# Attention and soft mixture of experts on one core: the first peaks by TensorE, fewer heating products, another order of tasks, idle products in two waits

## The chip, the core and the metric

The kernel runs on one core of one Trainium2 chip. The core has TensorE (PE: products of matrices, with PEld for the loading of weights), VectorE (DVE), ScalarE (ACT), GpSimd (POOL) and SyncE (SP), which here issues nearly all DMA transfers; 16 DMA engines move the data between the device's memory (HBM) and the core's SBUF. TensorE writes its results into PSUM. Every engine takes its instructions in the order in which they stand, and waits where an operand isn't there or a buffer isn't free. The metric is the device time of one execution in microseconds.

## What is computed

Two steps, in fp32 at the borders. First attention over 8 batches and 8 heads, 576 positions of 64 elements, with rotary embedding; then a soft mixture of 8 experts with 4 slots each, over 4608 rows of 512 elements.

```
q_rot, k_rot = rotate(q), rotate(k)
scores = scale * q_rot @ k_rot.T
scores = scores - max(scores, axis=-1)
attn = exp(scores); attn /= sum(attn, -1) + 1e-9
out = attn @ v                       # [8, 8, 576, 64]

x = out, with heads side by side      # [4608, 512]
logits = x @ phi                      # 32 slots
d = softmax(logits, axis=0)           # over the rows
slot_input = d.T @ x                  # [8, 4, 512]
for e in range(8):
    slot_out[e] = relu(slot_input[e] @ w1[e]) @ w2[e]    # 512 -> 1024 -> 512
c = softmax(logits, axis=1)           # over the slots
result = c @ slot_out                 # [4608, 512]
```

## The kernel before

Heads go in pairs, two heads of 64 elements over the 128 partitions: 32 pairs p, four to a batch (NP = 4). A pair passes through some 45 tasks, each a Python function that issues a few instructions on its engines. Its x_in (queries and keys, two transfers of 576 KB, L247, `load0` and `load1`, two buffers) is multiplied with cosine and sine by GpSimd (`spin0`, `spin1`, L253, eight operations), added by VectorE (`join`, L257), cast to fp16 by ScalarE (`high0`, `high1`, L262), and VectorE subtracts the cast from the original (`low`, L270), so that a number is held as two fp16 parts, hl. `low` is the last reader of x_in, so it frees the buffer.

The scores are made twice. The first time only to find the largest of each row: `m0` to `m4` and `m_rem` (L300, L313) form products into PSUM and VectorE reduces them (L303, L315); `m_min` (L319) joins the parts to nm, the negated maxima, one row per partition. TensorE turns nm (`m_turn`, L325), ScalarE scales and casts it to mr (`m_half`, L335), and two small DMAs on SP lay mr out over two partitions of the tile peak (`m_rows`, L340, L341). There are two such tiles, for even and odd pairs. The second time, `t0` to `t4` and `t8` (L355, L368 to L370) form the scores out of both parts, and a product of peak and the constant lift subtracts the maxima in PSUM; ScalarE takes the exponentials (L358, L373). Then follow the products with the values (`av0` to `av10`, L411, L422), the copies out of PSUM (`o_out`, `o_down`), `recip`, `norm`, the turning of the normalized result (`natural`, copied by ScalarE in `natural_out`, L474), and the pair's part of the logits (`logits`, L481, L484, added up by VectorE, L493). Per batch there are tasks for the running maxima and the slots. TensorE has three PSUM slots in rotation for all these tasks (`bank2`).

What stands where on each engine comes from the tables WHEN (the pairs in the middle), FIRST (the first five) and LAST (the last four): `at` turns task and pair into a number, `line` sorts the numbers, and a loop calls the tasks in that order. So the order of the calls is the order on TensorE, VectorE and ScalarE. In the function called `first_rows`, the first pair's `m_rows` is followed on SP by the loads of pair 2, of phi and of sel.

Before the loop the kernel forms products that nobody reads, to keep TensorE at work while the first pair's data come: `heat(N_WARM)`, 17 products (L759) at the start, and `heat(N_HEAT)`, 12 more ahead of the first `m_turn`.

The experts' weights are 64 tiles of 512 KB (L612). Thirty go into a pool wp during the pairs (`weights`). The others wait for space: wx (five tiles) and wk and wh1, wh0 for the buffers of the pairs' inputs and of hl, wq (five tiles) for the buffers of the last pairs (`release_fore`; one of them is peak), wl (four tiles) for those of the attention (`release_att`). `trickle` issues the ones of wx, wk and wh. `steady` is the list of instructions whose place on SP and GpSimd is set by the program that gathers them; it is closed ahead of the last `trickle` loop. The remaining loads take tiles that the first layer of the experts has read.

Behind the last pair come its `norm`, `natural` and `logits`, the statistics, the update of the slots (TensorE products L821 to L865, with a few products of lift and lift, L818, whose numbers SPEND gives, in the waits), the first layer (L889, four blocks of 32 products, the first block over the tiles 0 to 7; tile 6 is that of wk), the second (L910), and the combination (L938, L939), whose 18 tiles of 512 KB are stored by SP (L941).

Of the kernel before, what the change touches and what calls it, by code (L numbers as in the profile page):

```python
# [7 lines left out]
F32 = mybir.dt.float32  # L8
# [36 lines left out]
SPEND = (0, 4, 2, 0, 6)  # L45
STEPS = (0, 0, 5, 0, 0, 5, 0, 0, 0)
N_WARM = 17
N_HEAT = 12
# [20 lines left out]
    "m_min": (-3.52783, -3.74988, -3.4456, -3.54521), "m_turn": (-2.65751, -3.22757, -2.90005, -2.93818),  # L69
    "m_half": (-2.47643, -2.32388, -2.50442, -2.74079), "m_rows": (-1.67456, -1.59636, -1.01091, -1.36182),  # L70
# [10 lines left out]
    "o_out": (3.92962, 3.94615, 3.87859, 3.96882), "o_down": (4.02285, 3.90092, 4.43108, 4.25105),  # L81
    "weights": (6.68793, 8.11001, 10.4734, 7.96367), "recip": (7.06685, 8.50895, 7.64337, 5.66094),
    "norm": (9.04517, 9.97761, 7.81794, 8.82978), "soft3": (10.71329, -1.23258, 22.11176, 22.86781),
    "natural": (11.03659, 10.57574, 10.30017, 9.50469), "natural_out": (11.0413, 10.59331, 11.08607, 9.87664),
    "logits": (11.6819, 12.18299, 11.9393, 11.08074), "logits_sum": (11.75168, 12.37214, 12.01238, 11.24891),
    "stat1": (14.20481, 16.70567, 26.85987, 14.34257), "soft2": (17.19783, 18.68756, 28.52708, 15.06539),
    "slots": (24.26839, 14.86922, -21.6337, 15.49421), "soft0": (29.66187, 31.16378, 41.9456, 13.09224),
    "stat0": (58.67023, 6.43439, 39.30635, 12.92594),
}
FIRST = {  # L90
    "m_rem": (-420.74199, -258.52084, -165.95497, -91.55186, -32.58086),
    "m0": (-416.09865, -286.81487, -140.59459, -101.97371, -50.62576),
    "m2": (-412.20094, -270.0157, -129.84012, -87.82755, -68.19657),
    "m3": (-403.90776, -262.95985, -149.84108, -109.9302, -38.36104),
    "m1": (-399.15564, -289.81588, -118.56698, -106.41711, -36.28915),
    "m4": (-389.35943, -247.90996, -158.73441, -94.61606, -57.50848),
    "m_min": (-377.37328, -241.64993, -117.64569, -87.38313, -27.82539),
    "join": (-377.36326, -348.95641, -243.7818, -151.58901, -94.91012),
    "m_turn": (-352.2095, -226.16715, -100.92287, -72.642, -26.10801),
    "m_half": (-349.91816, -225.0694, -96.54795, -70.71858, -22.59302),  # L100
    "low": (-346.40436, -295.64275, -150.94049, -69.26017, -71.53601),
    "m_rows": (-337.67967, -197.52355, -88.5627, -36.46158, -4.19543),
    "t8": (-314.59698, -151.13586, -85.2923, -25.75504, -0.50974),
    "t2": (-311.27385, -151.13883, -84.94182, -0.14828, -0.87715),
    "t0": (-285.00525, -136.70424, -61.87914, -32.66543, -2.39072),
    "soft0": (-267.48427, -201.24595, 3.73945, 13.40987, -248.89171),
    "av5": (-267.32619, -96.76236, -76.7603, 1.06239, 0.13262),
    "t1": (-261.10481, -138.41608, -84.62048, -0.67329, -1.38994),
    "load_v": (-259.92437, -147.90602, -94.1895, -72.03072, -5.71268),
    "av1": (-258.00393, -93.30542, -37.73087, -16.69992, 3.26102),  # L110
    "av10": (-248.07756, -85.59323, -27.88133, 2.16407, 3.9268),
    "soft1": (-235.02539, -134.85944, -322.53084, 20.01567, 1.89106),
    "high0": (-234.98804, -340.48244, -222.89928, -142.08461, -85.55401),
    "t3": (-230.41978, -121.38007, -60.9526, -22.48296, -3.97013),
    "t4": (-229.99713, -146.42219, -62.60678, -23.05545, -3.99833),
    "soft3": (-222.15667, 24.22066, -12.56887, 24.46301, -39.84925),
    "av3": (-197.83158, -112.42151, -73.01473, 1.26269, -0.18588),
    "av4": (-194.34117, -111.6644, -39.4965, 1.16011, 2.88299),
    "av7": (-193.53141, -102.7179, -34.84723, -13.08601, 0.91351),
    "av9": (-192.59135, -134.50116, -32.79874, -14.28511, 1.64504),  # L120
    "av0": (-185.07388, -88.05057, -39.19938, 0.99983, -0.12547),
    "av8": (-170.0289, -94.63629, -56.43594, -14.16475, 2.53229),
    "av2": (-168.0465, -130.44334, -56.1101, 1.41561, 1.66757),
    "av6": (-155.12663, -95.29877, -39.5128, -4.51807, 3.20444),
    "o_out": (-147.40069, -82.01871, -26.27853, 2.29791, 4.03845),
    "load0": (-141.97913, -25.42989, -149.95166, -283.06751, -158.47656),
    "o_down": (-136.55419, -81.65478, -26.47399, 2.44084, 4.1333),
    "weights": (-109.57446, 25.46476, 6.62982, -1.59969, -58.15807),
    "recip": (-102.27546, -58.4345, -7.54993, 2.78188, 4.50588),
    "spin1": (-93.90425, -414.42416, -264.72383, -160.57665, -110.78333),  # L130
    "soft2": (-93.41299, -315.28447, -101.43259, 21.6938, -17.79966),
    "norm": (-90.51137, -31.67471, 5.54815, 7.84989, 6.27133),
    "natural": (-69.97429, -27.4891, 8.73388, 9.34029, 10.87984),
    "natural_out": (-59.04176, -25.9581, 9.65759, 9.79417, 11.06854),
    "logits": (-43.36981, 3.87649, 9.8946, 11.1204, 14.12073),
    "logits_sum": (-43.2881, 4.82347, 10.33544, 11.30244, 14.2095),
    "stat0": (-36.38519, 17.61955, 9.89016, 13.35178, -409.00246),
    "spin0": (-21.4379, -398.65092, -288.22025, -246.63741, -156.13304),
    "load1": (-6.95274, -271.47629, -100.89511, -206.15958, -156.77186), "trickle0": 0.4431, "trickle1": 1.2621,
    "trickle2": 2.5296, "high1": (3.15516, -324.01766, -205.53181, -139.88352, -73.53007), "trickle3": 3.4658,  # L140
    "stat1": (13.43099, -353.9255, 23.26806, 14.22494, -112.62711),
    "slots": (25.91835, -21.11139, -68.31089, 17.77357, -247.82112),
}
LAST = {
# [32 lines left out]
def attn_softmoe(ctx, tc, qk, q0, v, phi, w, cs, ident, sel, seg, out):  # L177
# [43 lines left out]
    for t in peaks:  # L221
        nc.vector.memset(t, 0.0)
# [816 lines left out]
```

## Time and profile before

| what | value |
|---|---|
| median of 3 runs | 506.17 us (503.56 to 509.76) |
| the profiled execution | 507.91 us, its span 506.1 us |
| TensorE busy | 478.3 us, 95% of the span |
| VectorE busy | 362.5 us, 72% |
| ScalarE busy | 290.6 us, 57% |
| GpSimd busy | 265.4 us, 52% |
| moved by DMA | 93.96 MB, 186 GB/s over the span |

The times of the rows below are microseconds from the start of the span. A line of the timeline has the start, the duration, engine, line of the kernel and operation, output and inputs with the sizes, and how many instructions of that kind stand together; in brackets stands how long the engine was idle before them and for what it waited. "SPq" is the queue of SP, whose DMA issues count here. PEclk is the clock that TensorE was granted, as a share of 2.4 GHz.

### The profile page before, as it was taken

How to read it: one execution, taken by the hardware profiler on the slowest of the kernel's cores; microseconds unless marked ns; L12 is line 12 of the kernel's file. 1: busy time of each engine (PE TensorE's matmuls, PEld its weight loads, DVE VectorE, ACT ScalarE, POOL GpSimd, SP SyncE). 2: the span in 40 equal slices, each digit the busy share in tenths (PEclk: the TensorE clock that was granted, in tenths of full speed). 3: DMA queues.
4: the chain of work that ended last, by engine and by line, in shares of the span. 5: the costliest groups of instructions: out<-in, count | busy, mean ns of one | idle time of the engine just before them, and what ended most of it. 6: DMA issues, size and time to landing. Idle time of an engine off the chain costs nothing. (4 is left out here: it accounts for less than half of the span.)

```text
span 506.1 us, 24787 instructions
## 1 busy us (share of the span) xinstructions
PE 478.3 (95%) x11269; PEld 377.9 (75%) x11269; DVE 362.5 (72%) x497; ACT 290.6 (57%) x522; POOL 265.4 (52%) x330
## 2 busy tenths in 40 slices
PE   4799999999999999999999989999999999899993
PEld 2577778878887888788778867887787886753872
DVE  5879879887788788777788668868887761236453
ACT  2355565675657666766676565765566555424442
POOL 3496697945954576458536845576657201120000
PEclk9999999999999999999999999999999999979998
DMA  7325553343544355434544444355335537579888
GB/s 265 127 96 184 212 188 126 122 166 122 206 164 166 122 191 180 157 126 168 204 123 141 136 179 146 125 190 182 128 139 167 187 100 296 199 272 408 330 349 334
DMA packets 27721, 93.96 MB, mean 186 GB/s; under 512 B 4064, under 2 KB 4320, under 8 KB 27616
## 3 DMA queue, kind: packets, MB, share of 16 engines
q1 hardware_dynamic: 27328, 91.79, 50.5%
q8 instruction: 88, 1.44, 1.1%
q10 hardware_dynamic: 288, 0.59, 0.3%
q14 instruction: 17, 0.14, 0.1%
HBM read 82.85 MB, written 9.44 MB: 182 GB/s over the span
## 5 line engine op out<-in xcount | busy, mean ns | idle before, releaser
L253 POOL TENSOR_TENSOR x_in<-x_in,cs_sb 128x288 f32<-128x288 f32 x248 | 206.1, 869 | 106.7 <-DMA x_in<-in_qk 76.0
L303 DVE TENSOR_REDUCE segs<-s_ps 128x14 f32<-128x896 f32 (+1 forms) x160 | 173.6, 1113 | 52.9 <-PE s_ps L300 48.4
L411 PEld LDWEIGHTS o_ps<-v_in,a_t 128*64 128x64 f32 x4608 | 147.1, 137 | 18.4 <-issue 16.6
L411 PE MATMUL o_ps<-v_in,a_t 128*64 128x65 f32 x4608 | 159.2, 224 | 0.9 <-issue 0.6
L358 ACT ACTIVATE a_t<-s_ps 128x896 f32<-128x896 f32 (+1 forms) x160 | 139.5, 943 | 23.3 <-PE s_ps L355 21.1
L355 PE MATMUL s_ps<-hl 64*128 64x448 f16 (+5 forms) x1536 | 121.6, 283 | 0.9 <-DVE segs L303 0.7
L355 PEld LDWEIGHTS <-hl 64*128 64x128 f16 x1536 | 71.8, 94 | 24.5 <-issue 2.0
L451 POOL TENSOR_TENSOR xn<-o_sb,rr 128x512 f32<-128x512 f32 x31 | 33.3, 1075 | 61.3 <-DVE rr L447 47.8
L355 PE MATMUL s_ps<-peak,lift 64*128 64x128 f16 (+5 forms) x512 | 59.3, 283 | 1.2 <-DMA peak<-mr 1.2
L300 PE MATMUL s_ps<-hl 64*128 64x448 f16 (+5 forms) x512 | 56.4, 286 | 0.6 <-DVE segs L303 0.5
L373 ACT ACTIVATE a_rem<-s_ps 128x640 f32<-128x640 f32 x32 | 22.8, 713 | 54.4 <-PE s_ps L370 54.4
L262 ACT CAST hl<-x_in 128x576 f16<-128x576 f32 x62 | 40.6, 673 | 17.0 <-DVE x_in L257 16.9
L270 DVE TENSOR_TENSOR hl<-x_in,hl 128x1152 f16<-128x1152 f32 x32 | 47.6, 1488 | 1.4 <-ACT hl L262 1.3
L257 DVE TENSOR_TENSOR x_in<-x_in 128x1152 f32<-128x1152 f32 x31 | 46.4, 1497 | 2.7 <-POOL x_in L253 2.7
L474 ACT COPY xt<-s_ps 128x576 f32<-128x576 f32 x32 | 20.4, 637 | 43.6 <-PE s_ps L325 43.6
L355 PEld LDWEIGHTS <-lift 64*128 64x128 f16 x512 | 25.9, 94 | 9.8 <-DMA peak<-mr 1.6
L422 PE MATMUL o_ps<-v_in,a_rem 64*64 64x65 f32 x1152 | 29.3, 223 | 3.0 <-issue 2.9
L300 PEld LDWEIGHTS <-hl 64*128 64x128 f16 x512 | 23.7, 95 | 8.8 <-issue 1.9
L315 DVE TENSOR_REDUCE segs<-s_ps 128x2 f32<-128x576 f32 x32 | 24.1, 754 | 7.7 <-PE s_ps L313 7.4
L422 PEld LDWEIGHTS o_ps<-v_in,a_rem 64*64 64x64 f32 x1152 | 25.2, 134 | 4.7 <-issue 4.6
L437 ACT COPY o_sb<-o_ps 128x585 f32<-128x585 f32 x31 | 20.2, 653 | 10.8 <-PE o_ps L422 5.3
L493 DVE TENSOR_TENSOR l_sb<-s_ps,l_sb 128x192 f32<-128x192 f32 x24 | 8.6, 357 | 22.4 <-PE s_ps L484 22.4
(156 smaller groups left out, 536.2 us busy)
## 6 DMA issues: line engine op xcount, KB each, us to landing
x_in<-in_qk SPq DMA_DIRECT2D x62, 576.0 KB
w_exp<-in_w SPq DMA_DIRECT2D x64, 512.0 KB
v_in<-in_v SPq DMA_DIRECT2D x32, 325.0 KB
out<-w_exp SPq DMA_DIRECT2D x18, 512.0 KB
x_in<-in_q SPq DMA_DIRECT2D x4, 288.0 KB
cs_sb<-in_cs ACTq DMA_DIRECT2D x2, 288.0 KB
peak<-mr SPq DMA_DIRECT2D x32, 2.0 KB
peak<-mr SPq DMA_DIRECT2D x32, 0.2 KB
```

The costliest lines, as they stand in the source:

```text
L253: eng.tensor_tensor(out=x[:, :, c], in0=x[:, :, c], in1=cs_sb[:, h, :, at:at + c.stop - c.start], op=ALU.mult)
L257: nc.vector.tensor_tensor(out=x[:, :, 0], in0=x[:, :, 0], in1=x[:, :, 1], op=ALU.add)
L262: nc.scalar.copy(out=halves[p][:, 1 + t], in_=loaded[p][:, t, 0])
L270: nc.vector.tensor_tensor(out=o, in0=x, in1=i, op=ALU.subtract)
L300: nc.tensor.matmul(s[:, h, at], lhsT=hl[rows[h], QH, P * j:P * j + P], rhs=hl[rows[h], KH, cols], start=True, stop=True)
L303: nc.vector.tensor_reduce(out=segs[p % 2][:, 0:8 * SG].rearrange("p (h c) -> p h c", h=2)[:, :, at:at + n // D], in_=s[:, :, 0:n].rearrang ...
L315: nc.vector.tensor_reduce(out=segs[p % 2][:, 8 * SG:8 * SG + 2], in_=s[:, :, 0:HC], axis=AX.X, op=ALU.max, negate=True)
L355: nc.tensor.matmul(s[:, h, at], lhsT=lhs, rhs=rhs, start=(w == 0 and at.start == 0), stop=(w == 3), skip_group_check=True)
L358: nc.scalar.activation(out=a, in_=s[:, :, 0:n], func=AF.Exp, scale=SCALE)
L411: nc.tensor.matmul(o, lhsT=ats[p, k][:, h, b:b + D], rhs=vts[p][:, 2 * i + h], start=(opening[p, h] == u and c not in begun), stop=(closin ...
L422: nc.tensor.matmul(o, lhsT=rems[p][r, at:at + D], rhs=vts[p][r, 8 + h], start=(opening[p, h] == REM and (h, c) not in begun), stop=(closin ...
L451: eng.tensor_tensor(out=x[:, 0:4].rearrange("p j h d -> p h j d"), in0=o[:, 1:9, 0:D].rearrange("p (h j) d -> p h j d", h=2), in1=rr[:, 1: ...
```

## The change

1. For the first pair, `m_turn` turns the maxima so that TensorE lays them out over the partitions of peak by itself: VectorE writes nm, scaled and cast, into a zeroed fp16 tile at_row at the two columns that belong to the two heads, six products with an fp16 identity bring them into PSUM, and ScalarE copies 128x576 elements into peak. The two DMAs of this pair are gone.
2. N_WARM goes from 17 to 12, N_HEAT from 12 to 6.
3. The loads of pair 2, of phi and of sel stand right behind the start instead of behind the first pair's `m_rows`.
4. The tables WHEN, FIRST and LAST have other numbers.
5. SPEND[0] goes from 0 to 16: 16 products of lift and lift stand ahead of the product that turns m_run. N_IDLE = 10 such products stand ahead of the logits of pair 30.
6. `steady` is closed behind the last `trickle` loop.

```diff
-SPEND = (0, 4, 2, 0, 6)
+SPEND = (16, 4, 2, 0, 6)
+N_IDLE = 10
-N_WARM = 17
-N_HEAT = 12
+N_WARM = 12
+N_HEAT = 6
 FIRST = {
-    "m_rem": (-420.74199, -258.52084, -165.95497, -91.55186, -32.58086),
+    "m0": (-798.68701, -282.09047, -202.25676, -140.56954, -56.98884),
+    "low": (-782.94014, -315.16537, -200.95702, -73.37034, -76.7725),
...
+    at_row = att.tile([P, 10, P], F16, name="a_rem", bufs=2)
+    nc.gpsimd.memset(at_row[:, 0:5], 0.0)
+    own = const.tile([P, 2], F32, name="own")
+    nc.vector.memset(own, 0.0)
+    for h in range(2):
+        nc.vector.memset(own[rows[h], h:h + 1], 1.0 / CM)
+    id_half = at_row[:, 5]
@@ m_min
+        if p == 0:
+            nc.vector.tensor_scalar_mul(out=at_row[:, 0:4, 0:65:64].rearrange("p j h -> p h j"),
+                                    in0=nm[:, 0:8].rearrange("p (h j) -> p h j", h=2), scalar1=1.0 / CM)
+            nc.vector.tensor_tensor(out=at_row[:, 4, 0:65:64], in0=nm[:, 8:9].broadcast_to([P, 2]), in1=own, op=ALU.mult)
@@ m_turn
+        if p == 0:
+            for j in range(4):
+                nc.tensor.matmul(t[:, 0, P * j:P * j + P], lhsT=at_row[:, j], rhs=id_half, start=True, stop=True)
+            for h in range(2):
+                nc.tensor.matmul(t[:, 1, 0:D], lhsT=at_row[:, 4], rhs=id_half[:, rows[h]], start=(h == 0), stop=(h == 1))
+            return
@@ m_half
+        if p == 0:
+            nc.scalar.copy(out=peaks[0], in_=flat.pop(p).rearrange("p n x -> p (n x)")[:, 0:S])
+            return
@@ m_rows
+        if p == 0:
+            return
@@ logits
-        flat["l", p] = lp = bank2()[:, 0]
+        s = bank2()
+        flat["l", p] = lp = s[:, 0]
+        if p == NPAIR - 2:
+            for _ in range(N_IDLE):
+                nc.tensor.matmul(s[:, 1, 0:P], lhsT=lift, rhs=lift, start=True, stop=True)
@@ the start and the end of the loop
-    def first_rows(p):
-        m_rows(p, nc.sync)
-        if p == 0:
-            do("load0", 2)
-            do("load1", 2)
-            nc.sync.dma_start(out=phi_sb, in_=phi.rearrange("(c p) n -> p c n", p=P))
-            nc.sync.dma_start(out=sel_sb, in_=sel)
     heat(N_WARM)
+    nc.scalar.copy(out=id_half, in_=id_sb)
     done.update((n, 0) for n in ("spin0", "spin1", "join", "high0", "high1", "load0", "load1"))
+    do("load0", 2)
+    do("load1", 2)
+    nc.sync.dma_start(out=phi_sb, in_=phi.rearrange("(c p) n -> p c n", p=P))
+    nc.sync.dma_start(out=sel_sb, in_=sel)
     p = NPAIR - 1
-    steady.close()
     while later:
         trickle(p)
+    steady.close()
     release_att()
```

What the new tables do at the start shows on VectorE, from the first reduction of pair 0 on (segs_127 is pair 0, segs_128 pair 1). Before:

```order
L315 TENSOR_REDUCE segs_127<-s_ps 128x2
L303 TENSOR_REDUCE segs_127<-s_ps 128x2x7 x3
L303 TENSOR_REDUCE segs_127<-s_ps 128x2x8
L303 TENSOR_REDUCE segs_127<-s_ps 128x2x7
L319 TENSOR_REDUCE nm<-segs_127 128x9
L270 TENSOR_TENSOR hl<-x_in,hl 128x2x576
L257 TENSOR_TENSOR x_in<-x_in 128x2x576
L270 TENSOR_TENSOR hl<-x_in,hl 128x2x576
L303 TENSOR_REDUCE segs_128<-s_ps 128x2x8
```

And of the change, where the lines of the same operations are 7 further down (segs_133 is pair 0, segs_134 pair 1):

```order
L310 TENSOR_REDUCE segs_133<-s_ps 128x2x7
L277 TENSOR_TENSOR hl<-x_in,hl 128x2x576
L310 TENSOR_REDUCE segs_133<-s_ps 128x2x8
L310 TENSOR_REDUCE segs_133<-s_ps 128x2x7 x2
L322 TENSOR_REDUCE segs_133<-s_ps 128x2
L310 TENSOR_REDUCE segs_133<-s_ps 128x2x7
L326 TENSOR_REDUCE nm<-segs_133 128x9
L329 TENSOR_SCALAR a_rem<-nm 128x2x4
L331 TENSOR_TENSOR a_rem<-nm,own 128x2
L264 TENSOR_TENSOR x_in<-x_in 128x2x576
L277 TENSOR_TENSOR hl<-x_in,hl 128x2x576
L310 TENSOR_REDUCE segs_134<-s_ps 128x2x7 x2
```

The subtraction of pair 0 (`low`) has moved from behind nm to the second place, and two small operations of the new way stand behind nm; the order of the reductions has changed too.

The other place is the end of SP's queue, from the last load of values on. peak_115 is the tile of pair 31. Before:

```order
L276 DMA v_in<-in_v 128x650
L612 DMA w_exp<-in_w 128x1024 x5
L340 DMA peak_115<-mr 2x4x128
L341 DMA peak_115<-mr 2x1x64
L612 DMA w_exp<-in_w 128x1024 x12
L875 DMA seg_in<-in_seg 128x320
L612 DMA w_exp<-in_w 128x1024 x17
L941 DMA out<-w_exp 128x1024 x18
```

And of the change:

```order
L283 DMA v_in<-in_v 128x650
L638 DMA w_exp<-in_w 128x1024 x2
L362 DMA peak_115<-mr 2x4x128
L363 DMA peak_115<-mr 2x1x64
L638 DMA w_exp<-in_w 128x1024 x17
L898 DMA seg_in<-in_seg 128x320
L638 DMA w_exp<-in_w 128x1024 x17
L964 DMA out<-w_exp 128x1024 x18
```

Two loads of weights instead of five stand ahead of the last peaks, and 17 instead of 12 behind them; in these 17 the five of wq now come first, and those of wx, wk, wh1, wh0 and wl follow.

## Rows read from the trace of the kernel before

**Rows 1.** Windows: length, each engine's busy us, PEclk, DMA share, GB/s.
```profile
17.60:20.50 2.90, 0.96 (x20) 0.55 (x21) 2.53 (x2) 0.61 (x2) 0.00 (x0) 1.00 0.02 6
24.00:420.00 396.00, 389.01 (x9776) 317.23 (x9777) 313.28 (x397) 249.76 (x438) 249.30 (x299) 1.00 0.46 157
456.00:476.00 20.00, 20.00 (x304) 11.46 (x297) 9.70 (x20) 8.29 (x20) 0.88 (x1) 1.00 1.02 406
498.00:504.30 6.30, 0.80 (x3) 0.19 (x1) 1.50 (x3) 0.86 (x2) 0.00 (x0) 0.91 1.01 401
```
**Rows 2.** Waits of PE from 24 to 420: us in total, times, longest.
```profile
PE o_ps L422 <- issue: 2.9, 3, 1.8
```
**Rows 3.** Timeline of the first 21 us, first pair.
```profile
6.54 4.24 PE L759 MATMUL s_ps<-hl,lift 128*128 128x288 f16 x17 [6.54 <-ACT hl L754]
...
11.44 0.76 DVE L315 TENSOR_REDUCE segs<-s_ps 128x2 f32<-128x576 f32 x1 [1.70 <-PE s_ps L313]
...
12.12 5.20 DVE L303 TENSOR_REDUCE segs<-s_ps 128x14 f32<-128x896 f32 x5
...
17.36 0.24 DVE L319 TENSOR_REDUCE nm<-segs 128x9 f32<-128x81 f32 x1
17.51 1.35 DVE L270 TENSOR_TENSOR hl<-x_in,hl 128x1152 f16<-128x1152 f32 x1
...
18.25 0.67 SPq L340 DMA_DIRECT2D peak<-mr  x1
...
20.50 0.32 PE L368 MATMUL s_ps<-peak,lift 64*64 64x320 f16 x1 [1.11 <-DMA peak<-mr]
...
28.62 0.24 DVE L319 TENSOR_REDUCE nm<-segs 128x9 f32<-128x81 f32 x1
```
**Rows 4.** All instructions of a line: ns min, median, max, first and last start.
```profile
L257 DVE TENSOR_TENSOR x_in<-x_in x31: 1302/1349/2199, 18.8 to 394.3; 128x1152 f32<-128x1152 f32 x31
L253 POOL TENSOR_TENSOR x_in<-x_in,cs_sb x248: 783/800/1937, 10.7 to 393.1; 128x288 f32<-128x288 f32 x124
```
**Rows 5.** Timeline of PE, pair 16 from turning to first peak product.
```profile
223.98 0.23 PE L325 MATMUL s_ps<-id_sb,nm 64*9 64x64 f32 x2
...
228.87 0.45 PE L355 MATMUL s_ps<-peak,lift 64*128 64x128 f16 x4
```
**Rows 6.** Timeline from 415 to 428, the peaks of pair 31.
```profile
415.85 6.13 SPq L612 DMA_DIRECT2D w_exp<-in_w  x5
...
421.00 4.59 PE L411 MATMUL o_ps<-v_in,a_t 128*64 128x65 f32 x144
...
422.08 0.54 SPq L340 DMA_DIRECT2D peak<-mr  x1
...
427.46 0.36 PE L355 MATMUL s_ps<-peak,lift 64*128 64x448 f16 x2 [1.20 <-DMA peak<-mr]
```
**Rows 7.** Timeline of two waits of PE behind the pairs.
```profile
439.00 0.64 ACT L474 COPY xt<-s_ps 128x576 f32<-128x576 f32 x1 [2.86 <-PE s_ps L325]
...
439.70 0.43 PE L481 MATMUL s_ps<-xt,phi_sb 128*32 128x128 f32 x8 [0.78 <-ACT xt L474]
...
443.22 0.29 PE L821 MATMUL t_ps<-id_sb,m_run 128*128 128x128 f32 x1 [1.21 <-DVE m_run L503]
...
443.35 0.39 PE L818 MATMUL t_ps<-lift 128*128 128x128 f16 x4
```
**Rows 8.** The clock behind them: a window, two blocks of the first layer.
```profile
446.00:452.00 6.00, 6.00 (x42) 3.82 (x38) 1.86 (x7) 0.82 (x2) 2.08 (x3) 0.50 0.70 277
449.81 4.71 PE L889 MATMUL a_ps<-w_exp,slot_t 128*32 128x512 f32 x32
...
454.81 3.64 PE L889 MATMUL a_ps<-w_exp,slot_t 128*32 128x512 f32 x32
```
**Rows 9.** The longest wait of SP before a load, and what followed.
```profile
SPq L612 <- PE s_ps L355: 10.4, 1, 10.4
434.44 5.93 SPq L612 DMA_DIRECT2D w_exp<-in_w  x8
```

More of the change, by code (lines that the diff above doesn't have):

```diff
@@ L84 @@
[L84 to L88, printed above, removed]
[4 rows of a table added]
+    "m_rem": (-9.7842, -5.55254, -5.99676, -6.16613), "low": (-8.94336, -10.34585, -10.06114, -8.95381),
[3 rows of a table added]
@@ new lines @@
+    "m_turn": (-3.32898, -3.38328, -3.55268, -3.11562), "m_half": (-2.52771, -3.35049, -3.37854, -3.10743),
[10 rows of a table added]
+    "o_out": (2.82184, 2.66131, 3.6385, 3.07031), "o_down": (3.14529, 2.38091, 3.58685, 2.87064), "trickle3": 3.4658,
+    "recip": (4.44305, 8.62887, 4.42739, 5.58412), "weights": (8.1384, 9.56048, 11.92387, 9.41414),
+    "norm": (8.42183, 9.23564, 5.50072, 8.28957), "natural": (9.69481, 9.5773, 8.64088, 8.82332),
+    "natural_out": (10.03513, 9.797, 8.87683, 8.82764), "logits": (10.87295, 10.97327, 10.79133, 9.38071),
@@ L89 @@
+    "logits_sum": (10.91132, 11.0979, 10.94056, 9.65926), "slots": (12.0362, 31.75839, 4.1585, 14.53382),
+    "stat0": (17.62091, 8.68106, 32.91044, 11.62621), "soft1": (18.51311, 37.58138, 8.71218, 14.88265),
+    "soft2": (31.99568, 74.85607, 29.00703, 17.8278), "soft0": (33.59811, 32.68813, 24.93532, 14.23654),
 }
 FIRST = {
[L91 to L93 removed]
@@ L94 @@
[L94 to L100, printed above, removed]
@@ new lines @@
+    "m_half": (-345.22896, -203.19863, -140.91902, -94.97933, -11.20616),
+    "m_rows": (-315.49635, -200.53709, -139.08662, -67.50312, -5.27356),
+    "t1": (-300.24851, -148.31206, -114.80845, -43.198, -4.30765),
+    "t3": (-292.3315, -173.71347, -96.13102, -34.3116, -1.86346),
+    "t4": (-280.86252, -162.61023, -102.54388, -53.17403, -1.4347),
+    "av2": (-270.55563, -121.94585, -54.61479, -6.56256, -0.5207),
+    "av6": (-269.5452, -122.42319, -83.20453, -8.8047, 1.59164),
+    "t0": (-265.08522, -178.14229, -90.55297, -62.95699, -4.12355),
@@ new lines @@
+    "av3": (-253.42537, -125.88456, -94.81468, -3.50564, 1.25638),
+    "t8": (-251.02894, -149.05201, -125.72827, -1.19809, -3.28098),
+    "stat1": (-246.13489, 0.75201, -594.94373, 13.84107, -39.85257),
+    "t2": (-245.59212, -176.83351, -87.54142, -44.05453, -1.62745),
+    "av7": (-233.83251, -126.11858, -87.30746, 1.50117, 1.44174),
+    "av8": (-232.25487, -121.8716, -68.66572, 0.92776, 1.6852),
+    "av0": (-225.15672, -141.51045, -71.01723, -19.69738, 1.69331),
+    "av4": (-217.91268, -156.31883, -54.44402, 1.33382, 0.03478),
@@ new lines @@
+    "av10": (-206.2555, -114.68106, -41.50273, 0.05665, -1.45173),
+    "av5": (-205.63326, -140.33706, -72.90071, -21.13184, -0.22305),
+    "av1": (-189.56341, -149.39064, -75.76832, -7.30826, 1.38258),
+    "av9": (-181.56208, -140.38154, -83.87385, -7.13008, -0.14452),
+    "o_down": (-181.03615, -113.25606, -33.01857, 1.8133, 2.79965),
+    "o_out": (-174.29627, -112.75719, -41.4095, 2.04172, 1.90569),
+    "recip": (-136.2414, -90.98847, 1.24573, 2.823, 6.14448),
+    "stat0": (-134.00598, -27.84756, -161.90459, 8.82697, -226.73399),
@@ new lines @@
+    "norm": (-127.71369, -23.71367, 4.9427, 4.87087, 7.86973),
+    "spin1": (-127.17566, -630.64109, -276.5106, -236.50887, -110.21109),
+    "high0": (-106.91482, -316.33251, -251.2306, -163.96779, -85.34597),
+    "soft1": (-103.90304, -768.61885, 28.26535, 15.55722, -82.39808),
+    "slots": (-93.54303, -101.4625, -90.52762, 14.57756, -108.94088),
+    "natural": (-82.17765, -21.30991, 5.01442, 4.8711, 9.74609),
+    "weights": (-79.24795, -13.07501, 35.71777, 16.13232, -80.43814),
+    "load0": (-74.4839, 9.5216, 25.22751, -321.92166, -188.86503),
@@ new lines @@
+    "natural_out": (-63.44267, 1.10457, 5.28505, 5.30629, 9.89163),
+    "soft2": (-61.2005, -235.95284, -126.81533, 21.25914, -643.60733),
+    "load1": (-59.56725, -273.91921, -71.83978, -281.94965, -164.65444),
+    "logits": (-59.52547, 4.91869, 5.6212, 6.2977, 10.66398),
+    "load_v": (-59.27776, -178.04136, -163.65529, -73.56077, -7.22405),
+    "logits_sum": (-53.02976, 6.67858, 5.71127, 6.35355, 11.37432), "trickle0": 0.4431, "trickle1": 1.2621,
+    "trickle2": 2.5296, "trickle3": 3.4658, "high1": (13.36634, -322.68395, -245.29784, -160.34372, -79.92352),
@@ L172 @@
+    "natural": (49.03514, 102.16183, 241.33158, -1.2391), "natural_out": (55.6206, 102.42264, 245.56008, -15.49135),
+    "soft0": (67.23181, -4.46006, -18.53984, -4.92821), "logits": (92.74409, 121.97648, 252.33327, -22.47652),
+    "logits_sum": (108.09832, 268.89274, 8.39787, -16.78847), "soft2": (124.36977, 139.91994, 0.45605, -16.79719),
 }
```

69 lines of the change are left out of this document (14 added, 55 removed), and 76 rows, old and new, of tables (LAST, WHEN).

## The prediction

> **What bounds the kernel now.** I read the busy times by stage first. From 24 to 420 us TensorE works 389.0 of 396 us while its granted clock stands at 1.00 and the DMA engines are busy 46% of the time [rows 1], so the pairs of heads in the middle cost what TensorE's products cost. The waits of that stretch come next: the largest line has 2.9 us in three stands, and they wait for nothing but issue [rows 2]. No change of order can win more there than the 7.0 us in which TensorE is idle. Behind 456 us TensorE is full too, and the DMA engines with it: 406 GB/s at a share of 1.02, and again 401 GB/s from 498 to 504.3, where nothing else works [rows 1]. The end is therefore a race between the chain of products and the last transfers, and a gain counts only if both get it. Last I read the start, where TensorE stands for whole microseconds, and the stretch from 420 to 455, where it waits three times and then runs at half its clock.
>
> **The start.** Before, the first products run 17 times, 6.54 to 10.78, 0.25 each [rows 3]. VectorE's first reduction starts at 11.44, six of them take 0.76 + 5.20, nm is ready at 17.60, then ScalarE and two DMAs follow, the first issued from 18.25, and the first product of peak and lift starts at 20.50: 2.9 us behind nm. In the change 12 products end at 6.54 + 3.0 = 9.54. m0.0 now stands first and needs three of the four casts; the first reduction stood 0.66 behind the last of the 17 products, so with 0.6 VectorE begins at about 10.15, 1.3 earlier. But low.0 stands second on VectorE, ahead of nm. It takes 1.35 alone; the same kind of operation reaches 1.94 and 2.2 where GpSimd multiplies beside it, and GpSimd's products stretch from 0.80 to 1.94 in their turn [rows 4]. I take 1.65, half way. So nm ends at 10.15 + 1.65 + 5.96 + 0.24 = 18.0, two small operations add 0.3 (a reduction over 81 elements takes 0.24), six products 0.5 with the hand-over (four of 128 columns took 0.39 [rows 7]), and ScalarE's copy of 128x576 takes 0.64, which a copy of that shape shows [rows 7]. The first peak product starts at 19.45, 1.05 us sooner. Waiting products of hl lie beside the copy and cost nothing.
>
> The Trainium skill ("SBUF — State Buffer", Who interferes with whom) says that a VectorE operation with two SBUF inputs and a GpSimd operation that reads SBUF exclude each other, the later one standing still for the whole of the other. The stretched maxima on both engines agree with it. By that rule alone low.0 would stand up to one GpSimd product longer, 0.80, so take 2.15, and the gain would be 0.55 instead of 1.05.
>
> The loads of pair 2 no longer stand behind the peaks on SP, and low.0 frees their buffer at about 13 instead of 18.9. GpSimd's next 16 products then start behind the first eight, near 17 instead of 23.58, beside join.1 and low.1, and join.2 moves ahead of nm of pair 1, 1.35 or more. That makes nm of pair 1 about 30.4 against 28.62 + 0.24 [rows 3], 1.5 late, and TensorE may stand 1 us for it; but join.2, which VectorE then has behind it, came later before. Bounds of the whole start: low.0 unstretched and the two small operations for nothing, 1.65; nm of pair 1 late by 1.5 with nothing got back, -0.5. I take 1.0, the price of the first peak product. Six heating products fewer lie in a wait and cost or win nothing; without them TensorE stands longer there, and its clock held 1.00 from 17.6 to 20.5 though it worked only 0.96 of 2.90 us [rows 1].
>
> **The middle.** The same products in another order cost the same. Counted from the order with the durations of the rows (an fp32 product of the values takes 4.59 / 144 [rows 6]), TensorE's work between the turning of the peaks and the first product that reads them was 4.9, 6.0, 7.1 and 8.0 us in the four pairs of a batch; it becomes 4.8, 4.4, 5.4 and 4.9. What must fit in is ScalarE's half, two issues and the landing. In pair 16 the trace has 224.21 to 228.87, 4.66 us, and no wait [rows 5]; at the start, with nothing else to do, nm to product took 2.90 with the turning, 2.25 of it from issue to product [rows 3]. So 4.4 should do. I take 0; the bounds are -6 (all waits gone) and +6 (a round of 5.0, 0.6 and 0.2 and 0.1 too long in three of four pairs).
>
> **The end of the pairs.** Before, five loads of 512 KB were issued from 415.85 on, 6.13 us long, and the peaks of pair 31 only at 422.08; the product that reads them waited 1.2 [rows 6]. Now two loads stand there, and the other loads behind. That wait goes: -1.2; the bounds are 0 and this.
>
> **Idle products.** logits of pair 30 waits 0.78 for a copy and the maximum of the slots 1.21 [rows 7]. Ten and 16 products of 128 columns fill them, at up to 0.1 each (four in 0.39): 1.0 and 1.6 at most, so 0.2 and 0.4 too long at worst, nothing at best. Behind these waits the granted clock falls to 0.50 from 446 to 452; the first block of 32 products takes 4.71 and the second, at 1.00, takes 3.64 [rows 8]. If the fill keeps the clock up, the first block saves 1.07. Ahead of it TensorE runs at half its clock from 446 to 449.8; half of these 3.8 us would be 1.9, but VectorE's steps lie between the products, so I take 1.1. Together -2.2 of TensorE's chain; the bounds are +0.6 (only the cost of the fill) and -3.0.
>
> **The loads of the weights.** SP stood 10.4 us before one load, for the last product that reads the peaks, and went on at 434.44 [rows 9]. Ten loads were then left; now 17 are, wq first, since the tiles of wx, wk and wh1 stand behind it in program order. TensorE is 2.2 earlier there (1.0 + 1.2), so the wait ends at 432.2. From 433 on, 17 + 17 loads, the small one and 18 stores of 512 KB are 27.4 MB, 67.3 us at 406 GB/s (1.29 for one): the last store lands at 500.4, against 504.3. The 11th load is the tile of the first block's third quarter: 433.1 + 11 x 1.29 + 0.5 = 447.8. The block starts at 449.8 - 4.4 + 1.1 = 446.5 and reaches that quarter at 448.3 on the full clock. It is just in time, and I take 0.3 for it.
>
> **Sum.** TensorE: -1.0 - 1.2 - 2.2 + 0.3 = -4.1. The transfers: -3.9 at most, -3.3 with 0.6 us for gaps between loads and stores. The later one decides: -3.3. The profiled execution took 507.91, so its counterpart takes 504.6. The median of the three runs is 506.17, 1.74 below that execution; from there the time is 502.9, and I say 503.0.
>
> **Rivals.**
> The clock falls anyway (15%): the fill then holds TensorE no busier than the waits allow, and 2.2 - 0.4 are lost from the chain: 503.0 + 1.5 to 2 = 505. For it: such products stood at 443.35 before too [rows 7], and the clock still fell. Against it: those came behind the wait, not in it.
> The start gains nothing (12%): VectorE, stretched by GpSimd, brings nm of pair 1 later; everything behind moves by 1: 504.
> The new order takes the waits of the middle (11%): -3, so 500. For it: 2.9 us of them are single stands; against it: they are waits for issue, not for a buffer.
> The loads behind one wait come too late (10%): the transfers run without a gap from 433 on, so each us by which the last read of the peaks is later than 432.2 goes into the end, and tile 6 stops the first block. With that read at 435.5, 3.3 later, the time is 506.
> Slower (6%): the round of the peaks no longer fits. In pair 31 issue to product took 5.4 us with loads beside it (422.08 to 427.46); with 0.4 ahead of it (0.65 from nm to issue at the start, less 0.23 for the turning) that is 5.8. If each round took so long, the pairs of the middle would miss 1.0, 1.4, 0.4 and 0.9 us, 27 of them 25 us: 528. It decides from 4.4 us on, and costs 2% from about 5.4. Against it: the loads of the pair stand 9 to 22 tasks ahead of the turning.
> Slower transfers (1%): each 10 GB/s below the 406 of the rows makes 27.4 MB last 1.7 us longer; at 360 the end is 8.6 later, 512. Against it: 406 holds over 20 us of loads, 401 over the last stores.
> The Trainium skill ("DMA: Bandwidth & Descriptors", Specifications) states some 358 GB/s of HBM for each core, by which the 27.4 MB would last an estimated 76.5 us; the trace disagrees, with 406.
>
> **How the numbers follow.** The likeliest case has 45%, with its own range of 501 to 505. About 2% is what a measurement of this kernel can tell from no change: 496.0 and 516.3. The range from 499 to 508 holds the first four cases and most of the fifth. Faster by over 2% takes all waits of the middle, the start's best bound and the clock together: 3%. Slower by over 2% is the upper half of the slow rival: 4%. Within: 93%.
>
> **What would show it.** The first peak product at 19.5 and nm of pair 1 near 30; no wait for peaks from 24 to 420, and none in pair 31; a granted clock of 1.00 from 445 to 452 and a first block of 3.7 us; no wait for a weight tile over 0.5; the DMA engines full from 433 to a last store near 501. It is wrong if TensorE's busy time in the middle changes by more than 1 us, if the peaks are waited for in many pairs, or if the transfers end later than 503.

## The result and the profile after

The changed kernel is slower: 509.96 us in the median of 22 runs (506.05 to 516.58), against 506.37 for the kernel before, also 22 runs. The ratio is 1.0073, with a 95% interval of 1.0048 to 1.0097, some 3.7 us. 503.0 was predicted, with a range of 499 to 508. The profiled execution took 512.26 us, its span is 510.5.

The first view is again that of the windows, for the stretches of [rows 1] and [rows 8] (length, busy time of PE, PEld, DVE, ACT and POOL, granted clock, share of the DMA engines, GB/s):

```profile
17.60:20.50 2.90, 2.06 (x22) 1.46 (x24) 2.56 (x5) 0.80 (x2) 2.90 (x3) 0.50 0.04 6
24.00:420.00 396.00, 387.01 (x9812) 317.31 (x9809) 308.19 (x394) 252.66 (x436) 240.12 (x290) 1.00 0.45 156
446.00:452.00 6.00, 4.38 (x36) 2.12 (x36) 1.18 (x5) 0.36 (x2) 1.68 (x2) 1.00 1.03 409
452.00:460.00 8.00, 5.40 (x22) 1.26 (x26) 0.94 (x2) 1.42 (x3) 0.00 (x0) 0.57 1.03 408
```

Three things are to be seen. TensorE is idle 9.0 us in the middle, where it was 7.0. From 446 to 452 its clock is at 1.00 now, as intended, where it was at 0.50. But in that window it works only 4.38 of 6 us, and behind it the clock falls after all. The timeline of TensorE shows why (start, duration, what it did, and in brackets how long it stood before and for what):

```profile
442.64 0.29 PE L844 MATMUL t_ps<-id_sb,m_run 128*128 128x128 f32 x1 [0.21 <-DVE m_run L529]
...
447.72 2.77 PE L912 MATMUL a_ps<-w_exp,slot_t 128*32 128x512 f32 x20
...
454.60 3.63 PE L912 MATMUL a_ps<-w_exp,slot_t 128*32 128x512 f32 x12 [4.12 <-DMA w_exp<-in_w]
```

The first block of the first layer starts at 447.72, 2.1 us sooner than before [rows 8]. After 20 of its 32 products it stands 4.12 us for a tile of weights: 20 products read the tiles 0 to 5, so the missing one is tile 6. (In the program a block is 16 products, and the trace records each twice: the 21st record is the first that reads tile 6.) The other 12 then run at the low clock, 3.63 us where 12 of a block at full clock take 12/32 of 3.64, 1.37. The block ends at 458.23; before it ended at 454.52. A lead of 2.1 us has become a lag of 3.7. The span is 4.4 longer.

SP's queue shows where the tile comes from (L638 are the loads of weights, L362 and L363 the peaks of pair 31):

```profile
422.50 0.54 SPq L362 DMA_DIRECT2D peak<-mr  x1
423.08 0.51 SPq L363 DMA_DIRECT2D peak<-mr  x1
434.15 18.20 SPq L638 DMA_DIRECT2D w_exp<-in_w  x17
453.35 0.33 SPq L898 DMA_DIRECT2D seg_in<-in_seg  x1
454.62 20.08 SPq L638 DMA_DIRECT2D w_exp<-in_w  x17
```

For 10.6 us, from 423.6 on, SP issues nothing. From 424 to 434 the DMA engines moved 205 GB/s before; here:

```profile
424.00:434.00 10.00, 9.60 (x235) 8.54 (x230) 0.57 (x2) 5.88 (x9) 3.54 (x6) 1.00 0.01 3
```

Then 17 loads come at once.

### The profile page after: what moved, and what is told of

It reads as the page before. It is cut to its first block, busy times and chain, and to the rows that moved or that the text cites. A ratio compares the mean times of both kernels' runs of the same rounds, so it can differ in the third digit from the quotient of the medians.

```text
span 510.5 us, 24805 instructions
## 1 busy us (share of the span) xinstructions
PE 478.7 (94%) x11288; PEld 378.6 (74%) x11288; DVE 360.2 (71%) x502; ACT 295.5 (58%) x523; POOL 268.0 (52%) x331
## 5 line engine op out<-in xcount | busy, mean ns | idle before, releaser
L433 PE MATMUL o_ps<-v_in,a_t 128*64 128x65 f32 x4608 | 157.6, 224 | 2.3 <-issue 2.2
L377 PEld LDWEIGHTS <-hl 64*128 64x128 f16 x1536 | 74.3, 95 | 21.8 <-issue 1.9
L473 POOL TENSOR_TENSOR xn<-o_sb,rr 128x512 f32<-128x512 f32 x31 | 34.5, 1114 | 54.4 <-DVE rr L469 37.1
L377 PE MATMUL s_ps<-peak,lift 64*128 64x448 f16 (+5 forms) x512 | 60.6, 285 | 0.2 <-issue 0.2
L269 ACT CAST hl<-x_in 128x576 f16<-128x576 f32 x62 | 39.3, 670 | 2.0 <-DVE x_in L264 2.0
L496 ACT COPY xt<-s_ps 128x576 f32<-128x576 f32 x32 | 20.5, 640 | 29.2 <-PE s_ps L336 28.7
L377 PEld LDWEIGHTS <-lift 64*128 64x128 f16 x512 | 27.4, 95 | 8.4 <-issue 0.9
L307 PEld LDWEIGHTS <-hl 64*128 64x128 f16 x512 | 22.4, 94 | 9.9 <-issue 0.8
L481 POOL TENSOR_TENSOR xn<-o_sb,rr 64x128 f32<-64x128 f32 x31 | 21.4, 689 | 2.4
```

The source lines that it names most:

```text
L269: nc.scalar.copy(out=halves[p][:, 1 + t], in_=loaded[p][:, t, 0])
L307: nc.tensor.matmul(s[:, h, at], lhsT=hl[rows[h], QH, P * j:P * j + P], rhs=hl[rows[h], KH, cols], start=True, stop=True)
L377: nc.tensor.matmul(s[:, h, at], lhsT=lhs, rhs=rhs, start=(w == 0 and at.start == 0), stop=(w == 3), skip_group_check=True)
L433: nc.tensor.matmul(o, lhsT=ats[p, k][:, h, b:b + D], rhs=vts[p][:, 2 * i + h], start=(opening[p, h] == u and c not in begun), stop=(closin ...
L473: eng.tensor_tensor(out=x[:, 0:4].rearrange("p j h d -> p h j d"), in0=o[:, 1:9, 0:D].rearrange("p (h j) d -> p h j d", h=2), in1=rr[:, 1: ...
```

## The experiments

All ratios are against the kernel before, run beside it on the same chip, with 95% intervals of 0.2% to 0.7% to each side. Several chips are in use, and two kernels that stood on different chips are compared by these ratios only. Theory A: the 17 loads behind one wait cost the time, through tile 6. Theory B: the new order costs it. Theory C: not that tile but the bytes left behind the wait.

**The closing of steady, undone in the change and done alone in the kernel before.**

```diff
+    steady.close()
     while later:
         trickle(p)
-    steady.close()
```

> The changed kernel with one part undone: steady is closed ahead of the trickle loop again, so that two of the loads for wx, wk and wh stand ahead of the last peaks on SP and six more between these and the first load of wq. All else as in the change. Theory A (the 17 loads behind one wait cost the time): the wait of 4.1 us for a weight tile in the first block of the first layer is gone, the clock stays at 1.00 there, and the time is 5 to 6 us below the change, 504.5, 0.995 to 0.997 of the kernel before. Theory B (the new tables and the new start cost it): no more than 1 us is won, and the ratio stays at 1.005 or above.

Measured: 1.0011 (0.9985 to 1.0036). The change itself was not run beside it; it has 1.0073 (1.0048 to 1.0097) above, and 1.0050 (1.0018 to 1.0083) in a second comparison, below, on this kernel's chip. So 0.4% to 0.6% come back, 2 to 3 us and not the 5 to 6 of theory A, and against the second comparison the intervals overlap. There is no wait for weights any more. The reverse edit, in the kernel before:

> The kernel before with this one part alone: steady is closed behind the trickle loop. Theory A: the first block waits some 2 us for tile 6, which lands about 20 us behind the first of the 17 loads; the last peaks come 1.2 us sooner; in all 1 to 4 us slower than before, 1.002 to 1.008. Theory B: nothing or a gain, 0.997 to 1.001.

Measured: 1.0062 (1.0030 to 1.0095). The first block of this kernel, which keeps the old order and all else, stands for the same tile at the same place:

```profile
446.30 2.77 PE L889 MATMUL a_ps<-w_exp,slot_t 128*32 128x512 f32 x20
...
451.18 2.35 PE L889 MATMUL a_ps<-w_exp,slot_t 128*32 128x512 f32 x12 [2.11 <-DMA w_exp<-in_w]
```

So this one part of the change costs some 0.6% by itself, and taking it back returns 0.4% to 0.6%. Theory B alone would have left both untouched.

**Is it the one tile, or the bytes?** First another tile in that place of the queue:

```diff
-WK = 6
+WK = 15
```

> The changed kernel with one number changed: the tile that is loaded 11th of the 17 is tile 15, which the second block reads, and no longer tile 6, which the first block reads. The loads and their bytes are the same. Theory A, if the lateness of that one tile is what costs: the first block runs through, the wait shrinks from 4.1 to below 1 us in the second block, and the time falls by 4 to 5 us to 505.5, 0.997 to 1.000 of before. Theory C (the bytes that are left behind the wait set the end, whichever tile is late): the wait goes but the end does not move, 509 to 510, 1.005 or above.

Measured: 1.0039 (1.0011 to 1.0068). The wait of 4.1 us is gone and the first block runs through in 3.64 (a wait of 0.9 us for weights in the second layer, L933, is there as in the change). But the time lies between the two forecasts, and against the change's 1.0050 on the same chip nothing can be told. Then the load of tile 6 ahead of the others, with the 16 left where they are:

```diff
         grow("wq", N_WQ)
+        i = next(i for i, x in enumerate(later) if x[0] == "wk")
+        name, bufs, n = later.pop(i)
+        load_w(hold[name], bufs, n=n)
         for _ in range(N_WQ):
```

> The changed kernel with one load moved: the one for tile 6 (wk) stands ahead of the five of wq instead of behind wq and wx; 16 loads stay behind the one wait. Theory A (one late tile): the load is issued right behind the last peaks, near 424, tile 6 is there, the first block runs through at 1.00 and the time falls by 4 us, 0.997 to 1.000 of before. Theory C (16 loads that start 10 us later set the end through their bytes, so the DMA engines stay full from 435 to the end): the wait is gone, but the time falls by 2 us only, 1.001 to 1.004.

Measured: 1.0011 (0.9980 to 1.0041). One load, issued at 425.38 rather than 442.90, goes with 1.0011 where the change has 1.0073 and 1.0050 (in other comparisons). The late tile is what stops the first block: there is no wait for weights any more. But 1.0011 lies in theory C's range and not in A's. The first block starts where it did before and runs at full clock, 1.07 us shorter, and the time is no shorter than before. The windows say what takes this back:

```profile
449.64 3.64 PE L915 MATMUL a_ps<-w_exp,slot_t 128*32 128x512 f32 x32
```
```profile
460.00:476.00 16.00, 16.00 (x287) 10.19 (x283) 7.13 (x14) 6.71 (x17) 1.32 (x2) 1.00 1.03 407
476.00:496.00 20.00, 19.02 (x356) 13.97 (x347) 10.12 (x19) 9.16 (x22) 0.00 (x0) 1.00 1.02 409
496.00:504.00 8.00, 2.68 (x9) 1.15 (x7) 3.32 (x5) 2.25 (x4) 0.00 (x0) 0.80 1.02 413
```

The DMA engines are full until 504 without a gap, and TensorE has run out of work by then. With the lateness of tile 6 gone the transfers set the end, so C holds for what is left.

**The wq loads last.** If early loads are good, all eight that can go early should:

```diff
         grow("wq", N_WQ)
-        for _ in range(N_WQ):
-            load_w(hold["wq"], N_WQ)
...
     while later:
         trickle(p)
+    for _ in range(N_WQ):
+        load_w(hold["wq"], N_WQ)
     steady.close()
```

> The changed kernel with the five loads of wq issued behind those of wx, wk, wh1 and wh0 instead of ahead of them; none of these moves ahead of the last peaks. Theory A: the loads start at about 424 instead of 434, tile 6 is the sixth and is there long before 447, no wait for weights, 503 to 504.5, 0.993 to 0.997 of before, the same as with the earlier closing or 0.5 better, since the last peaks have no load ahead. Theory B: 509. Theory C: 503 to 505 too, since fewer bytes are left behind the wait.

Measured: 1.0065 (1.0042 to 1.0089). A miss for A and C alike, and near theory B's 509, 1.0056 of 506.17; TensorE is idle 12.2 us here from 24 to 420. There is no wait for weights, but the first block starts only at 455.06, since TensorE stood twice on the way there, with the profile naming nothing that it waited for:

```profile
438.13 0.57 PE L444 MATMUL o_ps<-v_in,a_rem 64*64 64x65 f32 x20 [0.50 <-issue]
444.35 0.28 PE L336 MATMUL s_ps<-id_sb,xn 64*128 64x64 f32 x2 [2.19 <-issue]
```

The clock fell to 0.53 behind the second of them. The kernel that closed early has 0.82 at the place of the second. The change itself has neither, nor has the kernel before. Both kernels have the DMA engines at work from 430 to 434 us (shares of 0.93 and 0.99), where the change and the kernel before have 0.00 and 0.03. To see whether the transfers do it or the new order, I put transfers into the old one.

**Seven loads too many in the kernel before.** The tiles of wx, wk and wh1 are loaded twice:

```diff
+    again = []
     while later:
         trickle(p)
+        again.append(list(w_tiles)[-1])
+    for n in again[:7]:
+        nc.sync.dma_start(out=w_tiles[n], in_=w[n].rearrange("p (c f) -> p c f", c=2 if n < 4 * E else 4))
     release_att()
```

> The kernel before with seven loads too many: the tiles of wx, wk and wh1 are loaded a second time right behind the first time, ahead of the load that waits for the last read of the peaks (the same data into the same tiles; nothing else changes). Before, the DMA engines stood at 3% from 430 to 434. Theory D (transfers in flight make TensorE stand where the profile says issue): a stand for issue of about 2 us, which the kernel before does not have, appears between 425 and 446, as in the kernels that closed early with the new tables; the time rises by 2 us or more, 1.003 to 1.008 of before. Rival (those stands belong to the new tables): none there, 0.998 to 1.002.

Measured: 1.0112 (1.0048 to 1.0177). The timeline of TensorE and the windows:

```profile
436.66 2.32 PE L411 MATMUL o_ps<-v_in,a_t 128*64 128x65 f32 x71 [0.56 <-issue]
442.89 0.40 PE L325 MATMUL s_ps<-id_sb,xn 64*128 64x64 f32 x5 [2.44 <-issue]
```
```profile
424.00:434.00 10.00, 8.65 (x227) 6.80 (x225) 0.57 (x2) 4.54 (x7) 2.32 (x3) 1.00 1.01 397
436.00:444.00 8.00, 4.29 (x135) 3.68 (x132) 1.72 (x5) 1.72 (x3) 0.00 (x0) 0.97 1.03 408
444.00:452.00 8.00, 6.72 (x80) 4.77 (x80) 2.58 (x9) 2.16 (x9) 1.32 (x5) 0.50 0.99 394
```

Before, TensorE worked 6.0 us in 436 to 444, and no stand for issue lay there; with nothing added but transfers it stands 0.56 and 2.44. The clock, which before was at 0.57 from 444 to 452 and back at 1.00 behind it, stays at 0.50 until 460. So added transfers bring such stands without the new tables, and the rival is out. Full engines at the place of the stand are not enough, though: before, they have a share of 0.93 from 436 to 444. What is new is that they are full from 430 to 436 too.

What TensorE then lacks, the trace doesn't name, but the places say something. Between the two stands above lie 127 products and 127 loadings of weights (PEld), in the kernel with wq last 127 and 128. In all sixteen profiles, from 24 us to behind the first block, the 165 stands of TensorE for issue lie multiples of 255 such instructions apart, to within 7. And the page of the kernel before has a queue of its own for instructions:

```profile
PE 478.3 (95%) x11269; PEld 377.9 (75%) x11269; DVE 362.5 (72%) x497; ACT 290.6 (57%) x522; POOL 265.4 (52%) x330
...
q8 instruction: 88, 1.44, 1.1%
```

The 22538 instructions of TensorE over 88 packets are 256 to a packet. So the stands look like waits for the next packet of TensorE's own instructions, late behind the other transfers. That is argued from the counts; no run moved these packets alone. It would also account for the miss with wq last: loads issued early there are paid for by stands.

**The parts alone.** The idle products at the end, in the kernel before (SPEND[0] and N_IDLE as in the change):

> The kernel before with the idle products alone: 16 ahead of the turning of m_run, 10 ahead of the logits of pair 30. If the fill keeps the granted clock up, the stretch from 446 to 452 runs at 1.00 and not at 0.50, the first block of the first layer takes 3.64 instead of 4.71, it starts about 1.1 earlier, and the time falls by 2 us, 0.995 to 0.998 of before. If the transfers at the end hold it all the same, the first block is early but the ratio is 1.000; if the clock falls anyway, 1.000 to 1.001.

Measured: 0.9987 (0.9962 to 1.0012). The clock holds and the first block takes 3.64:

```profile
450.02 3.64 PE L894 MATMUL a_ps<-w_exp,slot_t 128*32 128x512 f32 x32
```

The reverse, on the kernel that closes early (SPEND[0] = 0, N_IDLE = 0):

> The changed kernel with steady closed early again and without the 26 idle products. If these keep the clock up, the stretch ahead of the first layer falls to 0.50 again and the time is 1 to 2 us above the same with them (1.0011), 1.003 to 1.005 of before; if they do nothing in this order, 1.001.

Measured: 1.0050 (1.0019 to 1.0081), against 1.0011 (0.9985 to 1.0036) with them, on another chip. Its first block:

```profile
453.86 5.64 PE L912 MATMUL a_ps<-w_exp,slot_t 128*32 128x512 f32 x32
```

That looks like some 2 us, but the intervals overlap, and this kernel also stood 2.19 us for issue on the way, where the one with idle products stood 0.82. Nor are the idle products all that decides. Of the six profiles without them the clock fell ahead of the first layer in four (blocks of 4.71, 4.84, 5.59 and 5.64), and held in two with the same waits of 0.78 and 1.21: the closing alone, above (20 products in 2.77), and the tables alone, below:

```profile
458.85 3.64 PE L888 MATMUL a_ps<-w_exp,slot_t 128*32 128x512 f32 x32
```

With them it held in all eight profiles that had no stand for issue over 1 us on the way. So they help as far as was seen, but a single pair of profiles does not show it; in the kernel before what they are worth can't be told from nothing.

The tables alone, in the kernel before (WHEN, FIRST and LAST exchanged):

> The kernel before with the new tables of the order alone; the peaks of the first pair go by DMA, no other idle or heating products. Theory B (the new order of the middle costs 2 to 5 us, in waits for issue and for peaks that the old order has less of): TensorE is idle 9 to 12 us from 24 to 420 instead of 7, 1.003 to 1.008 of before. Theory A (only the loads behind the one wait cost): 0.997 to 1.001.

Measured: 1.0136 (1.0099 to 1.0173), more than either theory gave. The new tables put join.2 ahead of nm of pair 1 on VectorE; with the old start the loads of pair 2 stand behind the first peaks, so nm of pair 1 comes at 35.10 instead of 28.86, and ScalarE's cast is waited for 3.7 us. The tables need the new start. The start alone, with the old tables:

> The kernel before with the new start alone: first peaks by TensorE, 12 and 6 idle products, loads of pair 2 early, old tables, old end. With the old tables low.0 stands behind nm, so VectorE reaches nm as early as 17 and the first peak product should start near 19, 1.5 us sooner than 20.50; 0.996 to 0.999 of before. If the earlier multiplications of GpSimd stretch VectorE's work as in the changed kernel, nothing is left: 0.999 to 1.002.

Measured: 1.0010 (0.9981 to 1.0038); the first peak product stands at 20.56, against 20.50, and not near 19. It isn't GpSimd's stretching either: low.0, behind nm, took 1.35 as before. nm ended at 18.21, against 17.60; two of the reductions ahead of it waited for products, 0.5 us in all. And the change itself beside them:

> The changed kernel itself, beside the parts on the same chip. Expected 1.005 to 1.009 of before, with a wait of about 4 us for a weight tile in the first block and 8 to 12 us idle of TensorE from 24 to 420.

Measured: 1.0050 (1.0018 to 1.0083), with a wait of 2.8 us for the tile, and TensorE idle 11.2 us from 24 to 420.

**More heating products.** N_WARM and N_HEAT back to 17 and 12, with steady closed early, with the load of tile 6 first, and with the old tables, new start and idle products:

> The changed kernel with steady closed early again and 17 and 12 heating products instead of 12 and 6. In three of seven profiles with 12 and 6 the granted clock fell to 0.50 for 3 to 7 us between 14 and 23 us. With 17 and 12 it should stay at 1.00 there; what that is worth is the question: up to 1 us against the same without it (1.0011), so 0.998 to 1.001 of before; nothing if VectorE sets the pace of the start.

> The changed kernel with the load of tile 6 ahead of those of wq and with 17 and 12 heating products. If the fall of the clock in the start costs TensorE's chain, 0.997 to 1.000 of before (1.0011 without the heating products); if VectorE sets the pace there, 1.000 to 1.003. No wait for tile 6, no stand for issue between 425 and 446, since the DMA engines are nearly idle from 426 to 434.

> The old tables, the old closing of steady and 17 and 12 heating products, with the peaks of the first pair by TensorE, the early loads of pair 2, and the idle products at the end. If the new tables are of no use by themselves, this is the best version: 0.996 to 0.999 of before. If the new tables carry the gain of the new start, 1.000 to 1.002.

Measured: 1.0035 (1.0002 to 1.0068), 1.0019 (0.9978 to 1.0059) and 1.0027 (0.9996 to 1.0058). The first two have counterparts of 1.0011 on other chips, so neither wins. The first, like the kernel with wq last, has a stand of 2.2 us for issue behind 420, with loads in flight. The clock of both is at 1.00 from 17.6 to 20.5, as it should be; of the seven profiles of the new tables and the new start with 12 and 6, five have 0.50 to 0.74 there. But nm of pair 0 ends at 18.88 and 18.89, against 18.16 and 18.08 in the counterparts, and the first product that reads the peaks starts at 20.57 and 20.51, against 20.75 and 20.50: what the clock wins behind nm, the added products cost ahead of it. The third has that product at 19.10, 1.40 sooner than before, and still its time can't be told from that of the kernel before. No version beat the kernel before beyond its interval.

## Why the prediction was wrong, point by point

**The loads of the weights: the step that failed.** It read "The 11th load is the tile of the first block's third quarter: 433.1 + 11 x 1.29 + 0.5 = 447.8." The rate is right: 409 GB/s from 446 to 452. The landing is not: TensorE goes on at 454.60, 6.8 us later. Single issues of the 17 loads, one from each of three narrow windows:

```profile
442.90 0.33 SPq L638 DMA_DIRECT2D w_exp<-in_w  x1
```
```profile
444.20 0.33 SPq L638 DMA_DIRECT2D w_exp<-in_w  x1
```
```profile
445.49 0.33 SPq L638 DMA_DIRECT2D w_exp<-in_w  x1
```

The 11th, 12th and 13th go out 1.30 apart, the time of one transfer. It looks as if from the ninth on each load waits until the load eight places ahead of it has landed: the 19th transfer goes out at 454.62, right behind the landing of the 11th (the 18th is the small one). The 11th, issued at 442.90, so takes 11.7 us from issue to landing, nine transfers' time.

Three things make the 6.8 us. The loads begin at 434.15 and not at 433.1: 1.05. The engines are not full at once, 247 GB/s over the 5.85 us to 440, where I had 406: 2.3. And by 454.60 they have moved 360 GB/s over 20.45 us, 7.4 MB, 14 loads and not 11: three loads' bytes belong to the ones behind the 11th, which are under way beside it: 3.9. From their sum comes off the 0.5 that I had for the landing. I had counted the loads as landing one by one at the full rate. So there is the stand of 4.1 us and the low clock behind it, 2.3 us, instead of 0.3. The windows:

```profile
434.15:440.00 5.85, 5.73 (x180) 5.14 (x178) 1.99 (x6) 1.95 (x4) 0.87 (x1) 1.00 0.73 247
434.15:454.60 20.45, 15.59 (x305) 11.10 (x303) 6.29 (x21) 4.91 (x14) 3.95 (x8) 0.96 0.94 360
```

The wait of SP itself ended 0.3 us sooner than before and not 2.2, since the start and the middle did not give what the sum had from them, as told below.

The rival of the loads that come too late named this tile and a price of 506, with 10%. The part of its mechanism that is about tile 6 is what was seen; its condition, a last read of the peaks at 435.5, was not met (434.15), and its transfers without a gap were not there. Its price was too low for the same reason as above.

**The transfers' sum was too tidy.** 67.3 us for 27.4 MB holds only if the engines run full to the end. In the change they do not (335 GB/s from 476 to 496): tile 6 holds up TensorE, and with it the stores. With tile 6 first they do, from 446 to 504, and then take back what the clock gave.

**Idle products: as forecast, but in part luck.** The clock stood at 1.00 in front of the first layer in every kernel that had them and no stand over 1 us for issue on the way, and the start of the first block moved up 1.8 us against the end of SP's wait (449.81 - 434.44 before, 447.72 - 434.15 now), where 1.1 was forecast. But the clock held without them too in two profiles of six, so the 0.50 of the kernel before, on which the term rests, was not certain to come. The gain of -2.2, with the first block's 1.07, was lost behind the missing tile.

**The start: a size that was off.** nm was forecast to end at 18.0 and ended at 17.91; low.0 took 1.69 where I took 1.65. The rows of the start, to be read beside [rows 3]:

```profile
11.15 1.69 DVE L277 TENSOR_TENSOR hl<-x_in,hl 128x1152 f16<-128x1152 f32 x1
...
11.60 1.90 POOL L260 TENSOR_TENSOR x_in<-x_in,cs_sb 128x288 f32<-128x288 f32 x1
...
17.67 0.24 DVE L326 TENSOR_REDUCE nm<-segs 128x9 f32<-128x81 f32 x1
...
18.02 0.36 DVE L329 TENSOR_SCALAR a_rem<-nm 128x8 f16<-128x8 f32 x1
18.28 0.15 DVE L331 TENSOR_TENSOR a_rem<-nm,own 128x2 f16<-128x2 f32 x1
...
19.19 0.64 ACT L352 CAST peak<-s_ps 128x576 f16<-128x576 f32 x1 [8.19 <-PE s_ps L345]
...
20.34 0.63 PE L377 MATMUL s_ps<-peak,lift 64*128 64x128 f16 x4
...
30.97 0.24 DVE L326 TENSOR_REDUCE nm<-segs 128x9 f32<-128x81 f32 x1
```

Two small operations and six products take 1.28 us instead of 0.8, and the product that reads the peaks stands 0.5 behind the end of the copy, since products of hl stand ahead of it and were not done. Gained: 0.16 of the 1.05. Six heating products fewer were not free either: the clock is 0.50 from 17.6 to 20.5, where nothing was counted for it. In the profile with tile 15 in the place of tile 6 it was at 1.00, and the product stood at 20.02, 1.94 behind nm and not 2.43. But restoring them won nothing, as told above. nm of pair 1 came 2.35 later, against 1.5 forecast.

By the rule of the Trainium skill ("SBUF — State Buffer", Who interferes with whom) low.0 would take up to an estimated 2.15; it took 1.69. The trace agrees with the rule: low.0 began 0.30 behind the start of a GpSimd product of 0.78 and took 0.34 longer than alone, about the rest of that product; the next GpSimd product, from 11.60 on, took 1.90 instead of 0.79 and ended behind low.0. The whole product of the 2.15 is the bound, and the forecast's 1.65, half way, was a guess that came out.

**The middle: not nothing.** Peaks were waited for twice, 1.4 us in all, so the slow rival hit only in passing. But nine profiles with new tables and new start have 8.9 to 12.6 us idle of TensorE from 24 to 420, 10.4 in the mean; six with the old tables have 7.0 to 9.4, 8.1 in the mean (profiles of several chips). The stands for issue make 8.2 and 5.4 us of these. TensorE's busy time there changed by 2.0 us, and over 1 us was a sign that the prediction named for being wrong. The stands lie at the same distances of 255 instructions as those of the reloads. That the new order puts transfers where they make TensorE stand is only argued, from the reloads; for the middle it was not tried, and stays open.

**The peaks of pair 31: right.** No wait there; the first product that reads them started at 426.97, issue to product took 4.47, against 5.38 before [rows 6].

**The sum.** Forecast -3.3. With tile 6 in time, the rest of the change measures 1.0011 (0.9980 to 1.0041), so the forecast gain is not there either. By the profiles the start gave nearly nothing, the middle lost some 2 us, and the transfers that begin 10 us later take back part of the 2.2 of the clock; no run gives these shares one by one in time.

## What to carry to other kernels

When many loads are let go at once, ask when the one needed first lands if those behind it move bytes beside it, and not only what its number is in the queue; if it is urgent, it goes ahead of them. A load moved behind a wait costs twice, through the bytes that it leaves for the end and through what needs it first, and one moved to an idle stretch is not free if TensorE then stands for issue. A clock that rose or fell in one profile is to be looked up in several before a term is built on it. Parts of a change that were made together (an order and a start here) are to be priced together, since one of them alone may lose what both don't.

## What the runs showed of the hardware that I had not expected

- The 11th of 17 loads of 512 KB took 11.7 us from issue to landing, nine times its share of 409 GB/s; when it had landed, the engines had moved the bytes of 14.
- Transfers alone, without any change of the instructions' order on TensorE, made it stand 2.44 and 0.56 us for nothing that the profile names, and its clock then stood at 0.50 from 444 to 460 (before, 0.57 from 444 to 452 and 1.00 behind it); in all 1.1% of the time (0.5% to 1.8%).
- In sixteen profiles TensorE's stands for issue lie multiples of some 255 of its instructions apart; its instructions come to 256 for each of the 88 packets of the queue for instructions.
- Loads and stores together held 407 to 413 GB/s from 460 to 504 us, in the kernel with the load of tile 6 first.
